# Attention with a bucketed bias and a snake feed-forward block: a new order of loads and units in the opening

## The chip, the cores and the metric

The kernel runs on one core of a Trainium2 chip. The metric is the device time of one execution in microseconds. A run of the kernel before took 372.21 us (median of three; 371.96 to 372.55).

## The reference

Eight batches, eight heads, 576 positions and a head size of 64: attention with a bias that depends on the distance of key and query alone, and then, over all 4608 rows of 512 numbers, a feed-forward block with the snake function.

```python
scores = q @ k.T / sqrt(64) + bias_table[bucket(|i - j|)]   # buckets: 32, one column a head
attn = softmax(scores)
x = (attn @ v) -> rows of all heads                          # 4608 x 512
h = x @ w_in                                                 # 512 -> 2048
g = h + sin(alpha * h) ** 2 / (alpha + 1e-9)
out = g @ w_out                                              # 2048 -> 512, float32
```

All distances from 128 on share the last bucket. So the exponential of a score is taken without bias, and only where a key lies within 128 positions of the query is it multiplied by the exponential of the bias (less that of the last bucket, which cancels in the softmax). These factors are the band rows.

## The kernel before, in words

**Names.** A batch is t (0 to 7); a pair p (0 to 3) is two heads. A pair's scores are transposed, keys on the partitions. The first 512 keys make four blocks c of 128, and such a unit is called A. The last 64 keys of both heads share one unit C. The last 64 queries have units of their own (B and X), which for the first batch are put off into the second batch. Every unit goes the same way: TensorE makes scores (L691, through the helper at L458), ScalarE takes the exponential into the tile `u` (L708), VectorE multiplies the part near the diagonal by the band rows `m2r` (L739), and for unit C VectorE or GpSimd does this with `mhr` (L725). Then TensorE multiplies with the values (`vs` for the first 512 keys, `vhs` for the last 64) and a column of ones, VectorE normalises (L953 and L954) into `xn`, TensorE transposes this for the first batch (L1025), and a copy puts it into `xT` (L538 on ScalarE, L540 on VectorE). The feed-forward block takes 512 rows of `xT` at a time: 16 groups of four matmuls with `w_in`, a sine on ScalarE (L1069), a square on ScalarE or VectorE (L1076, L1078), a sum on VectorE (L1083), and then four output tiles of 16 matmuls each with `w_out`, which may be put wherever TensorE would idle.

**The opening**, which is all the change touches directly. Batch 0's queries and keys come in pairs of heads. Pair 0 is loaded as float32 into `nat0` by SyncE (L433), cast into `natb` by `cast0` on VectorE (keys L468; queries half on VectorE, L516, half on GpSimd, L517), transposed by TensorE with an identity (L551) and copied to `kT` and `qT` by VectorE (L540). Pairs 1 to 3 come through GpSimd's queue, which casts on the way (`load_pair`, into `nat1`); pair 3 is issued later than the others. GpSimd copies the last 64 keys into `kts` (L582). The bias table goes through two small matmuls and an exponential (L596); the resulting 8 rows `e_sb` (L606) are written to DRAM (L607) and read back by SyncE with overlapping strides: `m2r` for heads 0-1, 2-3 and 4-7 (`load_m2r`, L474), and `mhr`, half-shifted rows for unit C, by two loads of their own (`load_mhr`, L481). The values of batch 0 come in three ways: heads 0 and 1 as float32 by SyncE at the very start into `vst` (L420), then cast by GpSimd (`cast_v`, L423); heads 2 and 3 through GpSimd's casting queue (L415); heads 4 to 7 as float32 by SyncE behind the band rows, and cast. `vst` lies in the memory of `w_out16`, so `w_out` can be loaded only after the casts. GpSimd then starts `w_in` (L439) once a one-element copy `tick` (L634) has seen the last band rows, clears the second set of tiles (`clear`), and loads batch 1's queries and keys into `nat2`, then `w_out` (L444), then batch 1's values.

**What sets the order.** A planner in the kernel's own Python code (`Plan`) holds tasks with the engines that may do them, a cost for each, dependences, a priority and a time before which a task isn't placed (`nb`; the constants `T_...`). It walks through its own estimate of time from `T_START`, gives each engine the ready task that can start first, and among those within 0.02 us the one with the lowest priority number. What comes out is a fixed order of instructions on each engine. At run time an engine waits at the head of its order for whatever its next instruction needs; nothing overtakes. In the first 22 us of the plan it also puts in products with a tile of zeros (`zz`, `warm1`), which only keep TensorE running.

## Time and profile before

| What | us |
|---|---|
| Median of three runs | 372.21 |
| The profiled execution | 372.11 |
| Span of its trace | 370.2 |
| TensorE busy | 362.5 |
| ScalarE busy | 316.8 |
| VectorE busy | 257.0 |
| GpSimd busy | 92.0 |

The trace starts with the first instruction of the program; the difference between span and time lies around it. PE is TensorE's matmul row, PEld its weight loads, DVE is VectorE, ACT ScalarE, POOL GpSimd, SP SyncE; a q behind a name is that engine's queue, issuing a DMA. A timeline row gives start and length in microseconds, engine, line of the kernel, operation, output and input by the program's names, shapes and a count, and in brackets how long the engine had been idle and what ended that. A window row gives a stretch and, for each engine, its busy time and number of instructions in it, then TensorE's granted clock, the share of the DMA engines and what they moved. A matmul's row is longer than the time it holds up the next one, as matmuls are pipelined. The granted clock is 1.00 all along.

### The profile page before, as it was taken

To read this page: it belongs to the slowest core of one execution; us is meant where nothing else is said; L and a number is where in the kernel's file an instruction comes from. 1 tells how busy PE (TensorE), PEld (TensorE's weight loads), DVE (VectorE), ACT (ScalarE), POOL (GpSimd) and SP (SyncE) were. 2 spreads that over 40 slices of the span, in tenths; PEclk is the share of its full clock that TensorE was granted. 3 is DMA by queue.
4 is the path that set the end of the run, shared out by engine and by line. 5 is a ranking of instruction groups with operands and counts; after the bars stand their busy time and mean duration, and the time that the engine had idled before them with its cause. 6 is when DMAs were issued, how large, how long until landed. Compare 5 with 4: busy or idle time off the path is not lost.

```text
span 370.2 us, 8922 instructions
## 1 busy us (share of the span) xinstructions
PE 362.5 (98%) x3576; PEld 195.7 (53%) x3576; DVE 257.0 (69%) x557; ACT 316.8 (86%) x433; POOL 92.0 (25%) x133
## 2 busy tenths in 40 slices
PE   7989999999999999999999999999999999999996
PEld 3564545644555446774554456445566455444443
DVE  4797957588677967696759776886769665979000
ACT  3998999899997999899979998999979997999111
POOL 7487450073000900073005600280005000000000
PEclk9999999999999999999999999999999999999999
DMA  9989999699525993399719991699259121000212
GB/s 169 199 160 205 201 163 147 132 90 141 99 58 109 122 161 71 86 134 143 119 48 146 141 145 53 135 115 171 68 105 104 61 69 37 7 28 4 84 60 86
DMA packets 149114, 40.49 MB, mean 109 GB/s; under 512 B 137080, under 2 KB 143568, under 8 KB 149072
## 3 DMA queue, kind: packets, MB, share of 16 engines
q0 software_dynamic: 96032, 17.67, 59.1%
q1 hardware_dynamic: 52864, 22.16, 25.4%
q8 instruction: 28, 0.46, 0.5%
q10 hardware_dynamic: 176, 0.09, 0.1%
q14 instruction: 14, 0.11, 0.1%
HBM read 37.73 MB, written 16.56 MB: 147 GB/s over the span
## 4 chain that ended last, share of the span: by engine, by line
PE 91%; ACT 5%; issue 1%; DVE 1%; ACTq 0%
PE pb L458 90%; ACT u L708 2%; ACT s L1069 1%; ACT sq L1076 1%; DVE u L739 1%; PE pb L1025 1%; PE pb L557 0%; ACT kT L538 0%; ACT qT L538 0%; DVE qT L540 0%; PE pb L551 0%; DVE xn L954 0%; DVE zz L509 0%; ACT outs L538 0%; DVE rd L953 0%
## 5 line engine op out<-in xcount | busy, mean ns | idle before, releaser
L708 ACT ACTIVATE u<-pb 128x1024 f16<-128x1024 f32 (+1 forms) x146 | 137.4, 1016 | 8.2 <-PE pb L458 6.7
L458 PE MATMUL pb<-w_out,g 128*128 128x512 f16 (+2 forms) x592 | 138.8, 374 | 0.0
L458 PE MATMUL pb<-xT,w_in 128*128 128x512 f16 (+4 forms) x704 | 127.6, 340 | 0.0
L1083 DVE SCALAR_TENSOR_TENSOR g<-sq,inv_a,pb 128x512 f16<-128x512 f16 x144 | 101.0, 743 | 7.1 <-ACT sq L1076 2.8
L1069 ACT ACTIVATE s<-pb,alphaT 128x512 f16<-128x512 f32 x144 | 93.0, 694 | 11.6 <-PE pb L458 10.8
L458 PEld LDWEIGHTS <-w_in 128*128 128x128 f16 x704 | 64.8, 98 | 57.4 <-issue 0.3
L739 DVE TENSOR_TENSOR u<-u,m2r 128x512 f16<-128x512 f16 (+1 forms) x128 | 62.2, 491 | 35.7 <-ACT u L708 32.5
L458 PEld LDWEIGHTS <-g 128*128 128x128 f16 x592 | 53.9, 98 | 59.9 <-issue 5.0
L458 PEld LDWEIGHTS <-u 128*128 128x128 f16 x1152 | 43.4, 97 | 10.4 <-issue 4.6
L403 POOL COPY kt<-kT 64x256 f16<-64x256 f16 x12 | 5.0, 421 | 171.2 <-DMA kT<-staged_k 86.3
L1076 ACT ACTIVATE sq<-s 128x512 f16<-128x512 f16 x71 | 44.4, 638 | 1.2 <-DVE g L1083 0.3
L458 PE MATMUL pb<-v,u 128*128 128x65 f16 x1024 | 44.1, 193 | 0.3 <-DVE u L739 0.3
L458 PE MATMUL pb<-qT,kT 64*128 64x64 f16 (+1 forms) x512 | 41.5, 285 | 1.5 <-ACT u L708 0.7
L1078 DVE TENSOR_TENSOR sq<-s 128x512 f16<-128x512 f16 x73 | 30.2, 423 | 12.4 <-ACT s L1069 11.5
L954 DVE TENSOR_TENSOR xn<-pb,rd 128x256 f16<-128x256 f32 (+2 forms) x59 | 28.5, 483 | 2.0
L458 PEld LDWEIGHTS <-kT 64*128 64x128 f16 x512 | 16.3, 94 | 22.9 <-issue 15.9
L458 PE MATMUL pb<-vh,u 128*128 128x130 f16 x128 | 28.2, 221 | 0.0
L408 POOL DMA_DIRECT2D v<-in_v_dram x28 | 24.8, 897 | 4.5 <-DMA nat<-in_k_dram 2.7
L538 ACT ACTIVATE outs<-pb 128x512 f32<-128x512 f32 (+2 forms) x12 | 6.8, 569 | 19.9 <-PE pb L458 19.9
L953 DVE RECIPROCAL rd<-pb 128x4 f32<-128x4 f32 (+2 forms) x59 | 10.9, 185 | 12.4 <-PE pb L458 12.3
L1148 ACT ACT_TABLE_LOAD x15 | 19.2, 1283 | 0.3
L540 DVE COPY outs<-pb 128x512 f32<-128x512 f32 x25 | 17.1, 685 | 3.2 <-PE pb L458 3.2
(75 smaller groups left out, 186.6 us busy)
## 6 DMA issues: line engine op xcount, KB each, us to landing
out_dram<-outs SPq DMA_DIRECT2D x35, 256.0 KB, 2.7
v<-in_v_dram POOLq DMA_DIRECT2D x28, 128.0 KB, 4.9
staged_k<-in_k_dram POOLq DMA_DIRECT2D x6, 576.0 KB, 9.1
staged_q<-in_q_dram POOLq DMA_DIRECT2D x6, 576.0 KB, 12.5
w_in<-in_moe_w_in_dram POOLq DMA_DIRECT2D x4, 512.0 KB, 8.7
w_out<-in_moe_w_out_dram POOLq DMA_DIRECT2D x4, 512.0 KB, 15.1
w_out<-in_v_dram SPq DMA_DIRECT2D x6, 128.0 KB, 6.2
xT<-xn SPq DMA_TRANSPOSE x47, 2.8
```

Source lines behind the costliest of these rows:

```text
L408: nc.gpsimd.dma_start(out=vs[t % 2][:, c, :, 0:D], in_=vp[128 * c : 128 * c + 128],)
L458: nc.tensor.matmul(out=out, lhsT=lhsT, rhs=rhs, start=start, stop=stop)
L540: k_of(e).tensor_copy(out=o, in_=i)
L708: nc.scalar.activation(out=o, in_=x, func=AF.Exp, scale=0.125)
L739: nc.vector.tensor_tensor(out=io, in0=io, in1=m2[:, 2 * p : 2 * p + 2, x0 : x0 + hi - lo], op=ALU.mult)
L953: nc.vector.reciprocal(out=r, in_=x[:, :, :, D])
L954: nc.vector.tensor_tensor(out=xn[:, 0:n].rearrange("p c (z d) -> p c z d", z=2), in0=x[:, :, :, 0:D], in1=r.unsqueeze(3).to_broadcast([128 ...
L1069: nc.scalar.activation(out=s16.v, in_=h.v, func=AF.Sin, scale=alphaT[:, f : f + 1])
L1076: nc.scalar.activation(out=sq.v, in_=s16.v, func=AF.Square)
L1078: k_of(e).tensor_tensor(out=sq.v, in0=s16.v, in1=s16.v, op=ALU.mult)
L1083: nc.vector.scalar_tensor_tensor(out=gcell[b].v[:, f, :], in0=sq.v, scalar=inv_a[:, f : f + 1], in1=h.v, op0=ALU.mult, op1=ALU.add,)
L1148: nc.scalar.preload_act_table_set(name)
```

## The change

All six loads of pairs 1 to 3 are issued by GpSimd at the start. The first queries are cast whole by VectorE. The copy of the first keys out of PSUM may be done by ScalarE alone. The two `mhr` loads are gone: GpSimd copies those rows out of `m2r`, in three pieces (pair 0, pair 1, pairs 2 and 3), each two instructions, and the multiplies of unit C wait for their piece. All eight heads' values of batch 0 come as float32 by SyncE, each pair of them behind the band rows of its heads, and GpSimd casts all eight; every product with values waits for its own heads' casts. `vhs` of batch 0 is loaded earlier on GpSimd's queue. `tick` waits for the middle band rows instead of the last; `w_in` is four tasks that other work may come between. The clears are split in three and due at 7.5 instead of 24.5. Batch 1's queries and keys wait for all casts, and `w_out` follows in a task of its own.

The planner gets a start for each engine, other due times and costs, and `HEAD_PRI`, priorities for single tasks of the opening. From the orders before and after: pair 1's keys are transposed ahead of the first scores. Pair 3's two copies on VectorE stand ahead of the first band multiply. The exponentials of unit C come one or two places sooner. Four feed-forward matmuls stand before the last pair's products instead of two. From there on the instructions are the same, apart from places of output matmuls, small copies that changed engine (batch 1's transposed keys and queries: six on ScalarE and two on VectorE, before five and three), and three output matmuls that stand before batch 1's first scores.

```diff
-        free = {e: t0 for e in ("PE", "ACT", "DVE", "POOL", "SP")}
+        free = dict(t0)
...
-T_START = 4.0
+T_START = {"PE": 4.7, "ACT": 3.6, "DVE": 6.05, "POOL": 5.6, "SP": 3.0}
-T_W0 = 24.5
+T_W0 = 22.6
-T_WI = 16.8
-T_CL = 24.5
+T_WI = 16.2
+T_CL = 7.5
-T_FIRST = (4.75, 5.95)
-T_PAIR = ((7.9, 8.5), (9.3, 10.2), (11.6, 12.3))
-T_M2 = (13.0, 14.8, 16.0, 16.0)
-T_MH = 14.2
-T_RST = 25.0
+T_FIRST = (4.97, 6.15)
+T_PAIR = ((6.6, 7.7), (8.7, 9.7), (10.7, 11.8))
+T_M2 = (13.1, 15.1, 18.0, 18.0)
+T_MH = (13.15, 15.15, 18.05)
+T_RST = 23.5
+T_V0 = (13.7, 14.3, 15.9, 16.5, 18.9, 19.5, 20.2, 20.8)
-T_TR1 = (36.0, 39.0)
-T_WO = (40.5, 43.0, 45.7, 48.3)
+T_TR1 = (33.2, 37.2)
+T_WO = (39.1, 41.7, 44.3, 47.4)
+HEAD_PRI = {0: 5618.9, 1: 5618.8, 3: 3520.2, ...}
...
-    def load_mhr(eng):
+    def copy_mhr(p0, p1):
         for z in range(2):
-            eng.dma_start(out=mhr[64 * z : 64 * z + 64], in_=bass.AP(tensor=e_dram, ...))
+            r, x = slice(64 * z, 64 * z + 64), 192 - 64 * z
+            P_.tensor_copy(out=mhr[r, p0:p1], in_=m2r[r, 2 * p0 + z : 2 * p1 : 2, x : x + 192])
...
-    load_v32(0)
-    load_v32(1)
...
-    load_pair(1)
-    load_pair(2)
+    for p in range(1, NP):
+        load_pair(p)
...
-    cast0(0, nc.vector)
-    x0 = nat0[:, 1].rearrange("s two (i d) -> s i two d", i=SI)
-    nc.vector.tensor_copy(out=natb[:, 1, :, 0], in_=x0[:, :, 0])
-    P_.tensor_copy(out=natb[:, 1, :, 1], in_=x0[:, :, 1])
+    for kq in range(2):
+        cast0(kq, nc.vector)
...
-            eng = {"ACT": 0.65} if p in T_ACT and kq else {"DVE": 0.75}
+            eng = {"ACT": 0.62} if p == 0 and not kq else {"DVE": 0.75}
...
-            load_m2r(nc.sync, 0, 2, 0)
-            load_mhr(nc.sync)
-            load_m2r(nc.sync, 2, 4, 3)
-            load_m2r(nc.sync, 4, H, 4)
-            for h in range(4, H):
-                load_v32(h)
+            for h0, h1, r in ((0, 2, 0), (2, 4, 3), (4, H, 4)):
+                load_m2r(nc.sync, h0, h1, r)
+                for h in range(h0, h1):
+                    load_v32(h)
...
+        for i, (p0, p1) in enumerate(((0, 1), (1, 2), (2, NP))):
+            x = plan.add({"POOL": ...}, lambda e, p0=p0, p1=p1: copy_mhr(p0, p1), [], 9000 + 3 * i, nb=T_MH[i])
+            mdone.extend([x] * (p1 - p0))
+        for h in range(H):
+            vdone.append(plan.add({"POOL": 0.45}, lambda e, h=h: cast_v(h), [], 9001 + 1.1 * h, nb=T_V0[h]))
+        for i in range(3):
+            plan.add({"POOL": 0.8}, lambda e, i=i: clear(P_, 1, i), [], 9900, nb=T_CL)
...
-            P_.tensor_copy(out=tick, in_=m2r[0:1, 4, 0:1])
+                if i == 0:
+                    P_.tensor_copy(out=tick, in_=m2r[0:1, 2, 0:1])
+                load_w_in16(i // 2, (2 * (i % 2),))
...
+        x = plan.add({"POOL": 1.7}, lambda e: load_nat2(), [], 9022, nb=T_RST, after=[x] + vdone)
+        x = plan.add({"POOL": 3.2}, lambda e: load_w_out16(), [], 9022, nb=T_RST, after=[x])
...
-                             ds + prev + (vdone[2 * y : 2 * y + 2] if t == 0 and p > 1 else []),
+                             ds + prev + (vdone[2 * p : 2 * p + 2] if t == 0 else []),
...
+    for i, x in HEAD_PRI.items():
+        plan.tasks[i].pri = x
     plan.run(T_START)
```

More of the change, by code (lines that the diff above doesn't have):

```diff
@@ L727, in bd @@
                 )
-            d = plan.add({"POOL": 0.45} if t == 0 and p else {"DVE": 0.25 if two else 0.15}, bd, [x],
-                         base + 10, nb=late, use=[ub])
+            d = plan.add({"POOL": 0.45} if t == 0 and p else {"DVE": 0.25 if two else 0.15}, bd,
+                         [x] + (mdone[p : p + 1] if t == 0 else []), base + 10, use=[ub])
             for pp in (p, p + 1) if two else (p,):
```

81 lines of the change are left out of this document (34 added, 47 removed), and 11 rows, old and new, of the table HEAD_PRI.

## Prediction

> **What bounds the kernel now.** I read the busy times of the page first, then windows, then single engines' timelines where the windows show a change of limit. TensorE has 98% of the span. The windows below cut it where the first feed-forward product is nearly complete (29.41) and where the second table load begins (46.30).
>
> ```profile
> PE 362.5 (98%) x3576; PEld 195.7 (53%) x3576; DVE 257.0 (69%) x557; ACT 316.8 (86%) x433; POOL 92.0 (25%) x133
> ```
>
> ```profile
> core 0: us, PE busy (x) PEld busy (x) DVE busy (x) ACT busy (x) POOL busy (x), PEclk, DMA share, GB/s
> 1.27:29.41 28.14, 25.70 (x327) 15.16 (x328) 20.70 (x57) 21.62 (x27) 19.88 (x45) 1.00 1.05 186
> 29.41:46.30 16.89, 16.36 (x191) 8.31 (x189) 14.78 (x27) 16.23 (x30) 8.70 (x14) 1.00 1.24 203
> 46.30:370.20 323.90, 320.48 (x3064) 172.24 (x3063) 221.18 (x473) 278.95 (x377) 62.87 (x71) 1.00 0.82 98
> ```
>
> After 46.30 TensorE is busy 320.48 of 323.90 us: that stretch is a fixed amount of work and moves only with its start. Before 29.41 TensorE's records hold warming products with the zero tile too, and run into each other, so they don't say what paces it. The change is worth what it moves the first sine (30.46) and everything behind it. Which engine paces the opening is seen in ScalarE's timeline and in the window from 15 to 20.
>
> ```profile
> 8.10 10.89 ACT L708 ACTIVATE u<-pb 128x1024 f16<-128x1024 f32 x12 [1.01 <-PE pb L458]
> 19.26 3.35 ACT L708 ACTIVATE u<-pb 128x1024 f16<-128x1024 f32 x4 [0.27 <-PE pb L458]
> 23.21 1.02 ACT L708 ACTIVATE u<-pb 128x1024 f16<-128x1024 f32 x1 [0.61 <-PE pb L458]
> ...
> 24.40 2.44 ACT L708 ACTIVATE u<-pb 128x512 f16<-128x512 f32 x3
> ...
> 30.46 0.69 ACT L1069 ACTIVATE s<-pb,alphaT 128x512 f16<-128x512 f32 x1 [0.47 <-PE pb L458]
> ```
>
> ```profile
> 15.00:20.00 5.00, 4.34 (x53) 2.37 (x51) 4.96 (x13) 4.74 (x6) 1.92 (x6) 1.00 0.84 199
> ```
>
> ScalarE works through twenty exponentials from 8.10 to 26.84 (24.40 + 2.44) with two stalls, 0.27 and 0.61, both for scores from TensorE. VectorE meanwhile is full, 4.96 of 5 us. TensorE takes its instructions in order: a product with the values that waits for VectorE's band multiply holds back the scores behind it, and so VectorE's backlog becomes ScalarE's stall. From the last exponential to the first sine are 30.46 − 26.84 = 3.62 us, a chain of multiply, product, normalisation, transpose and copy whose links the change leaves.
>
> **The change part by part.**
>
> *First exponential.* The first queries are now cast whole by VectorE, and the first of the copies out of PSUM goes to ScalarE.
>
> ```profile
> 4.30 0.56 DVE L468 CAST natx<-natx 96x768 f16<-96x768 f32 x1 [1.52 <-DMA natx<-in_k_dram]
> 5.47 0.36 DVE L516 CAST natx<-natx 96x384 f16<-96x384 f32 x1 [0.61 <-DMA natx<-in_q_dram]
> ```
>
> ```profile
> 5.50 0.69 POOL L517 CAST natx<-natx 96x384 f16<-96x384 f32 x1 [1.16 <-DMA natx<-in_q_dram]
> 6.50 0.59 ACT L606 ACTIVATE e_sb<-pb 8x512 f16<-8x512 f32 x1 [0.46 <-PE pb L458]
> L538 ACT ACTIVATE kT<-pb 128x576 f16<-128x576 f16 x3 | 2.1, 707 | 0.0
> 6.86 0.76 DVE L540 COPY qT<-pb 128x576 f16<-128x576 f16 x1 [0.37 <-PE pb L551]
> ```
>
> The queries were ready at 5.50 + 0.69 = 6.19 and will be at 5.47 + 0.56 = 6.03: −0.16. With the two value loads gone from beside them they may land a little sooner: I take −0.2, bounds 0 and −0.4. Pair 1's key transposes now stand before the first scores; what hides them is the copy of the first queries, which ended at 7.62 and will end near 7.4. If pair 1's keys land after that, every tenth counts. On ScalarE the key copy (0.71) stands ahead of e_sb, whose wait of 0.46 hides part of it: 0.71 − 0.46 = +0.25 for all band rows, bounds 0 and +0.4.
>
> *Band rows and VectorE.* This is the largest term: VectorE's timeline, then two landings from the list of DMA issues (its last number).
>
> ```profile
> 12.57 0.76 DVE L540 COPY qT<-pb 128x576 f16<-128x576 f16 x1 [0.16 <-PE pb L557]
> 14.72 0.43 DVE L739 TENSOR_TENSOR u<-u,m2r 128x512 f16<-128x512 f16 x1 [1.39 <-DMA m2r<-e_dram]
> 15.06 0.75 DVE L540 COPY kT<-pb 128x576 f16<-128x576 f16 x1
> 15.73 0.75 DVE L540 COPY qT<-pb 128x576 f16<-128x576 f16 x1
> 16.39 1.01 DVE L739 TENSOR_TENSOR u<-u,m2r 128x768 f16<-128x768 f16 x2
> ...
> 17.55 0.65 DVE L739 TENSOR_TENSOR u<-u,m2r 128x512 f16<-128x512 f16 x1
> ```
>
> ```profile
> 27.00 0.41 DVE L739 TENSOR_TENSOR u<-u,m2r 128x512 f16<-128x512 f16 x1
> ```
>
> ```profile
> 10.06 0.37 SPq L474 DMA_DIRECT2D m2r<-e_dram  x1
> m2r<-e_dram SPq DMA_DIRECT2D x1, 192.0 KB, 4.6
> nat<-in_k_dram POOLq DMA_DIRECT2D x1, 144.0 KB, 3.5
> ```
>
> VectorE idles 1.39 for the rows and only then, with multiplies due, does pair 3's two copies (1.5). With all keys and queries issued at once these copies can follow pair 2's, which ended at 12.57 + 0.76 = 13.33: by 14.1 to 14.8, so in the idle gap or nearly. The rows, issued at 10.06, landed 4.6 later; now issued near 10.3 with less beside them, they take between 3.5 (the quickest load of similar size, pair 3's keys) and 4.6: 13.8 to 14.9. I take 14.5 for the start of the multiplies, nearer the row of the same load. Pair 0's five took 0.43 for the first and 18.20 − 16.39 = 1.81 for the others, 2.24, so they end at 16.75 where they ended at 17.55 + 0.65 = 18.20: −1.45 before any cost.
>
> *What GpSimd now does there.* It gets six half-shift copies in place of two DMAs, casts eight value heads where it cast six, and does its clears early.
>
> ```profile
> 17.45 0.47 POOL L725 TENSOR_TENSOR u<-u,mhr 128x128 f16<-128x128 f16 x1 [1.08 <-DMA mhr<-e_dram]
> 18.96 0.18 POOL L634 COPY tick<-m2r 1x1 f16<-1x1 f16 x1 [1.04 <-DMA m2r<-e_dram]
> ...
> 22.08 0.44 POOL L423 CAST v<-w_out 128x256 f16<-128x256 f32 x1
> ```
>
> ```profile
> 23.50 0.76 POOL L423 CAST v<-w_out 128x256 f16<-128x256 f32 x1
> ```
>
> GpSimd's multiply at 17.45 lay under VectorE's at 17.55, which took 0.65 where the one at 27.00 took 0.41: 0.24 a meeting. Four casts and four copies now run from about 14 to 19, among the multiplies. A copy's length no row shows; the cast's 0.44 is the nearest. Three meetings make +0.7; the bounds are 0 and eight whole ones, 8 × 0.44 = +3.5. I stay low since the cast at 23.50, at 0.76, shows GpSimd waiting in its turn. VectorE's net is −0.75. The Trainium skill, SBUF — State Buffer, section "Who interferes with whom", says that a VectorE operation with two SBUF inputs and a GpSimd one that reads SBUF exclude each other for a whole instruction. Both long rows agree; by the rule alone the term lies nearer its upper bound, and that case is a rival below.
>
> *Values as float32 behind the rows.* Two casting loads on GpSimd's queue become SyncE loads, and the two that went out first now stand behind the first rows.
>
> ```profile
> w_out<-in_v_dram SPq DMA_DIRECT2D x1, 128.0 KB, 6.3
> w_out<-in_v_dram SPq DMA_DIRECT2D x1, 128.0 KB, 4.2
> 16.74 0.22 PE L458 MATMUL pb<-vh,u 128*128 128x130 f16 x1
> 18.83 0.39 PE L458 MATMUL pb<-qT,kT 64*128 64x512 f16 x2
> ```
>
> Issued at about 10.7 and 11.2 (0.37 an issue and its gap), they land 4.2 to 6.3 later, the second between 15.4 and 17.5; with its cast it is ready between 15.9 and 17.9. The middle, 16.9, lies beside multiplies that end at 16.75 + 0.7 = 17.45 with meetings: hidden unless near its upper end. The first product with values, at 16.74 before, starts no sooner, but meets no copies behind it. The last rows, for pairs 2 and 3, stand behind four value loads instead of two half-shift loads. GpSimd saw them land at 18.96; pair 2's multiplies need them soon after. I take +0.2, bounds 0 and +0.5.
>
> *Weights.* GpSimd started w_in after that wait at 18.96; it now waits for the middle rows, and has no clears between casts and the second batch. All these loads start 1 to 3 us earlier. No link of the chain to the first sine is a wait for w_in, so I count nil; it keeps them ahead of what moves earlier.
>
> *Sum.* ScalarE starts at −0.2. Of its 0.88 of stalls, VectorE's −0.75 takes as much, less part of the +0.2: −0.8 at most, together −1.0 for the last exponential and the first sine (29.5). Two more feed-forward matmuls run before the last transposes, in time TensorE idled, but from 29.41 to 46.30 ScalarE is busy 16.23 of 16.89 and gets one copy more (0.71), which earlier output matmuls cover. I count these two as nil, ±0.4. The profiled execution took 372.11 (span 370.2): 371.1. The median of the runs shown is 0.1 above it: **371.2**.
>
> **The rivals.**
>
> *A larger gain.* Rows and copies are there at 13.8 to 14.1, both stalls vanish, the extra matmuls and the earlier start count in full: −0.4 − 0.88 − 0.6 = −1.9, 370.3. For it: the idle 1.39 and the moved 1.5 are more than I credit. Against: ScalarE has 17.9 of work from first to last exponential without stalls, so no more than that can go.
>
> *A wash.* VectorE's gain comes, but the late e_sb (0.25), the last rows (0.3) and ScalarE's extra copy (0.3) eat all but 0.2: 372.0. For it: ScalarE is near full in both stretches.
>
> *Slower: the first values come late.* TensorE stands at the first product, in order, with the scores that ran at 18.83 behind it. The values decide from a landing of about 17.7 on: ready 18.1, product 18.1, scores near 18.8 as before. From there each us is a us for ScalarE. At 18.9, when the last rows landed on this queue, it costs 1.2: 373.4.
>
> *Slower: whole exclusion.* Eight GpSimd operations take 0.44 each from VectorE: +3.5 − 1.45 = +2.1 there, of which half reaches ScalarE past the time it has in hand: 373.2. Against: the long cast.
>
> **How the numbers follow.** Forecast 0.42, larger gain 0.18, wash 0.20, late values 0.10, whole exclusion 0.10. 0.2%, 0.74 us, is about what a measurement here can tell from no change. Faster: 0.39 of the forecast's 0.42 and the larger gain, 0.57. Same: the forecast's near edge, 0.03, the wash, and 0.02 of the two slower cases, 0.25. Slower: what is left of these two, 0.18. The range begins at the larger gain, 370.2, and reaches over the wash to the near side of the two slower cases, 372.9.
>
> **What would show it.** Right: the first band multiply near 14.5 with pair 3's copies before it, the last exponential ending near 25.8, the first sine near 29.5, and behind it the same distance to the end. Wrong: a first product with values that GpSimd's cast releases after 17.9; VectorE multiplies of 0.8 beside GpSimd copies; ScalarE stalls that add up to 0.9 again; or TensorE idle after 46 us that was not there.

## The result, and the profile after

The changed kernel takes 374.57 us (median of six runs, 373.43 to 375.19) beside 372.38 for the kernel before in the same runs: 1.0059 times as long, 95% interval 1.0039 to 1.0078. It is slower by 2.2 us; the forecast was 371.2, within 370.2 to 372.9. The profiled execution took 374.60 with a span of 372.9. Medians stand below because some executions, of the kernel before too (19 of its 122 beside the experiments), take 375 us or more; the last section shows one.

First the windows of the changed kernel, cut at the first sine, at the second table load and at the end, and then the window from 15 to 20 (columns as before).

```profile
core 0: us, PE busy (x) PEld busy (x) DVE busy (x) ACT busy (x) POOL busy (x), PEclk, DMA share, GB/s
1.27:31.32 30.05, 27.34 (x330) 15.78 (x331) 21.93 (x55) 22.78 (x30) 24.55 (x53) 1.00 0.95 176
31.32:47.94 16.62, 16.11 (x177) 7.60 (x177) 14.63 (x25) 16.51 (x29) 6.82 (x13) 1.00 1.24 201
47.94:372.88 324.94, 321.12 (x3082) 171.79 (x3073) 222.45 (x475) 277.64 (x375) 62.53 (x69) 1.00 0.81 98
15.00:20.00 5.00, 3.09 (x41) 1.82 (x40) 4.50 (x9) 3.98 (x5) 4.29 (x9) 1.00 1.10 257
```

The first sine is at 31.32 where it was at 30.46, and from the second table load to the end there are 324.94 us where there were 323.90. So 0.86 us were lost in the opening and 1.84 of the span behind the first sine (341.56 us to the end instead of 339.72): 1.04 in the stretch that the prediction held to be fixed, and the other 0.8 between the first sine and the second table load, called the sine stage below. It takes 16.62 us with 29 instructions on ScalarE. Here is its window in the kernel before, where there are 28:

```profile
30.46:46.31 15.85, 15.36 (x186) 7.93 (x185) 14.79 (x27) 15.80 (x28) 7.66 (x13) 1.00 1.25 202
```

ScalarE is busy for nearly all of both (16.51 and 15.80 us). ScalarE's timeline shows the opening.

```profile
8.48 9.76 ACT L711 ACTIVATE u<-pb 128x1024 f16<-128x1024 f32 x11 [1.02 <-PE pb L468]
19.26 1.02 ACT L711 ACTIVATE u<-pb 128x1024 f16<-128x1024 f32 x1 [1.01 <-PE pb L468]
20.71 3.35 ACT L711 ACTIVATE u<-pb 128x512 f16<-128x512 f32 x4 [0.43 <-PE pb L468]
24.24 2.43 ACT L711 ACTIVATE u<-pb 128x512 f16<-128x512 f32 x3 [0.18 <-PE pb L468]
...
26.90 1.02 ACT L711 ACTIVATE u<-pb 128x1024 f16<-128x1024 f32 x1
```

Three stalls add up to 1.62 us (1.01, 0.43, 0.18) where two made 0.88. Each is a wait for scores. TensorE's waits from 4 to 30 us have these longest rows (total, times, longest):

```profile
PE pb L468 <- DVE u L742: 1.0, 1, 1.0
PE pb L468 <- POOL v L430: 0.7, 1, 0.7
```

TensorE stood first for GpSimd's cast of the first values, then for a band multiply, with the scores behind. The band rows were read late: SyncE's row for the first read, its landing, and GpSimd up to the start of `w_in`.

```profile
11.65 0.40 SPq L484 DMA_DIRECT2D m2r<-e_dram  x1
m2r<-e_dram SPq DMA_DIRECT2D x1, 192.0 KB, 3.8
```

```profile
15.46 0.96 POOL L492 COPY mhr<-m2r 64x192 f16<-64x192 f16 x2 [1.28 <-DMA m2r<-e_dram]
16.48 0.82 POOL L430 CAST v<-w_out 128x256 f16<-128x256 f32 x2
17.25 1.15 POOL L492 COPY mhr<-m2r 64x192 f16<-64x192 f16 x2
18.48 0.47 POOL L728 TENSOR_TENSOR u<-u,mhr 128x128 f16<-128x128 f16 x1
18.91 1.39 POOL L430 CAST v<-w_out 128x256 f16<-128x256 f32 x2
20.24 0.18 POOL L637 COPY tick<-m2r 1x1 f16<-1x1 f16 x1
20.37 2.17 POOL L446 DMA_DIRECT2D w_in<-in_moe_w_in_dram  x3
```

The read was issued at 11.65, not near 10.3. GpSimd is then full from 15.46, and the weights, which were to start earlier, start at 20.37, 1.2 us later than before. Behind the first sine TensorE now has a wait on a load (from 30 to 60 us) that the kernel before does not have:

```profile
PE pb L559 <- DMA nat<-in_k_dram: 0.5, 1, 0.5
```

The chain that ended last changed as well. Its lines, of the kernel before and of the changed one:

```profile
PE 91%; ACT 5%; issue 1%; DVE 1%; ACTq 0%
```

```profile
PE 87%; DMA 7%; POOL 4%; ACT 0%; issue 0%; DVE 0%; ACTq 0%
PE pb L468 86%; DMA w_out<-in_moe_w_out_dram 5%; POOL v L430 1%; DMA e_dram<-e_sb 1%; DMA m2r<-e_dram 1%; POOL mhr L492 1%; POOL w_out L451 1%; POOL w_in L446 1%; PE pb L1028 0%; POOL nat L440 0%; POOL u L728 0%; ACT e_sb L608 0%; ACT kT L540 0%; PE pb L553 0%; DVE zz L514 0%
```

Before, the chain ran over ScalarE's work in the opening and the sine stage (ACT 5%). Now it runs over the write and read of the band rows, GpSimd's copies and casts, and then the loads of `w_in` and `w_out`: 5% of 372.9 is some 19 us behind a load of `w_out`.

### The profile page after: what moved, and what is told of

It reads as the page before. It is cut to its first block, busy times and chain, and to the rows that moved or that the text cites. A ratio compares the mean times of both kernels' runs of the same rounds, so it can differ in the third digit from the quotient of the medians.

```text
span 372.9 us, 8932 instructions
## 1 busy us (share of the span) xinstructions
PE 364.6 (98%) x3575; PEld 195.2 (52%) x3575; DVE 259.3 (70%) x556; ACT 316.9 (85%) x434; POOL 94.5 (25%) x138
## 3 DMA queue, kind: packets, MB, share of 16 engines
q1 hardware_dynamic: 53376, 22.23, 24.5%
## 4 chain that ended last, share of the span: by engine, by line
PE 87%; DMA 7%; POOL 4%; ACT 0%; issue 0%; DVE 0%; ACTq 0%
PE pb L468 86%; DMA w_out<-in_moe_w_out_dram 5%; POOL v L430 1%; DMA e_dram<-e_sb 1%; DMA m2r<-e_dram 1%; POOL mhr L492 1%; POOL w_out L451 1%; POOL w_in L446 1%; PE pb L1028 0%; POOL nat L440 0%; POOL u L728 0%; ACT e_sb L608 0%; ACT kT L540 0%; PE pb L553 0%; DVE zz L514 0%
## 5 line engine op out<-in xcount | busy, mean ns | idle before, releaser
L742 DVE TENSOR_TENSOR u<-u,m2r 128x768 f16<-128x768 f16 (+1 forms) x128 | 64.4, 507 | 37.8 <-ACT u L711 36.2
L468 PE MATMUL pb<-qT,kT 64*128 64x64 f16 (+1 forms) x512 | 42.6, 285 | 0.6 <-ACT u L711 0.5
L1081 DVE TENSOR_TENSOR sq<-s 128x512 f16<-128x512 f16 x72 | 29.9, 424 | 12.5 <-ACT s L1072 11.6
L540 ACT ACTIVATE outs<-pb 128x512 f32<-128x512 f32 (+2 forms) x10 | 5.5, 554 | 19.9 <-PE pb L468 19.9
L542 DVE COPY outs<-pb 128x512 f32<-128x512 f32 x27 | 18.5, 685 | 2.0 <-PE pb L468 2.0
L956 DVE RECIPROCAL rd<-pb 128x4 f32<-128x4 f32 (+2 forms) x59 | 11.0, 186 | 12.3 <-PE pb L468 10.8
```

Source lines behind the costliest of these rows:

```text
L468: nc.tensor.matmul(out=out, lhsT=lhsT, rhs=rhs, start=start, stop=stop)
L542: k_of(e).tensor_copy(out=o, in_=i)
L742: nc.vector.tensor_tensor(out=io, in0=io, in1=m2[:, 2 * p : 2 * p + 2, x0 : x0 + hi - lo], op=ALU.mult)
L956: nc.vector.reciprocal(out=r, in_=x[:, :, :, D])
L1081: k_of(e).tensor_tensor(out=sq.v, in0=s16.v, in1=s16.v, op=ALU.mult)
```

## The experiments

The theories, in the letters of the texts on record. **W**: the write of `e_sb` to DRAM is seen to land only when loads issued ahead of it have landed; six loads ahead of it instead of four make the band rows late. **G**: GpSimd's reads and VectorE's band multiplies exclude each other. **V**: the first values come late. **S**: TensorE's order behind the first sine is tied to the weights' stream (`w_in`, batch 1's rows, `w_out`), which starts later, while the due times put its users earlier. **C**: the exponential's cost in the plan, 0.055 instead of 0.065, worsens the order of the later batches. One text speaks of the late pair as a pair of values; it is pair 3's keys and queries.

### One suspect of the opening at a time

Late fourth pair (W), in the changed kernel:

```diff
-    for p in range(1, NP):
+    for p in range(1, NP - 1):
...
-            plan.add({"POOL": 0.8}, lambda e, i=i: clear(P_, 1, i), [], 9900, nb=T_CL)
+            plan.add({"POOL": 0.8}, lambda e, i=i: (load_pair(3) if i == 0 else None, clear(P_, 1, i)), [], 9900, nb=T_CL)
```

> The changed kernel, but pair 3's two loads are issued where GpSimd begins its early clears, just behind the write of the band rows to DRAM, as in the kernel before; all else in the same order. Theory W: that write is only seen to land when the loads issued ahead of it have landed (11.43 in the changed kernel, then the first read at 11.65; 9.91 and 10.06 before). Then the first read is issued near 10.2, 1.4 us sooner, the first band multiply starts near 14.1 to 14.5, and the time falls by 0.8 to 1.4 us, to 373.2 to 373.8. Theory G, GpSimd's copies slow VectorE and that is what costs: the read moves but the time falls by less than 0.5. If the write is late only because of its own later start (7.49 against 7.12), the first read stays near 11.6.

Half-shifted rows by two loads again, no GpSimd copies (G):

```diff
+                if h0 == 0:
+                    load_mhr(nc.sync)
...
-            x = plan.add({"POOL": ...}, lambda e, p0=p0, p1=p1: copy_mhr(p0, p1),
+            x = plan.add({"POOL": ...}, lambda e: None,
```

> The changed kernel with the half-shifted rows loaded by two DMAs behind the first band rows as before, and no GpSimd copies of them; all orders otherwise the same. Theory G, a GpSimd copy that reads the fast memory and a VectorE multiply exclude each other: the multiplies from 15.5 to 20 fall from 0.56 to 0.78 to about 0.45 to 0.6, the value casts end about 1 us sooner, and the time falls by 1 to 1.5 us. Theory W (the late write costs): the multiplies get shorter, but values and later rows now land 0.6 to 1 us later behind the two DMAs, and the time changes by less than 0.5.

First two value heads loaded at the very start again (V):

```diff
+    load_v32(0)
+    load_v32(1)
     nc.scalar.preload_act_table_set(EXP_SET)
...
-                for h in range(h0, h1):
+                for h in range(max(h0, 2), h1):
```

> The changed kernel with the value loads of heads 0 and 1 issued at the very start as before; the order of all engines the same. Theory V, the first product waits for late values: TensorE's wait of 0.71 for the cast goes and the time falls by about 0.7. Theories W and G: the product then waits for VectorE's multiply instead, which ended at 18.2 anyway, so the time stays within 0.3, or rises a little, as these loads land among the keys and queries (first queries 0 to 0.2 later).

The kernel before with all pairs issued at once (W from the other side):

```diff
     load_pair(2)
+    load_pair(3)
...
-        plan.add({"POOL": 1.4}, lambda e: load_pair(3), [], 9001, nb=T_P3)
+        plan.add({"POOL": 1.4}, lambda e: None, [], 9001, nb=T_P3)
```

> The kernel before with pair 3's two loads issued together with the others at the start, and nothing else: all orders stay. Theory W: the write of the band rows, issued at 7.1, is seen to land only behind them, near 11.2 to 11.5 instead of 10.06; band rows and first multiply come 1 to 1.4 us later, and the time rises by 0.7 to 1.4 us. Without W the transposes of pair 3 have their data sooner and the time stays or falls by up to 0.4.

Measured beside 372.42 (the ratios are estimated by themselves and are not quotients of the medians): 374.41 with the late pair (ratio 1.0045, 1.0010 to 1.0080), 374.79 with the loads (1.0045, 1.0014 to 1.0076), 375.27 with early values (1.0075, 1.0035 to 1.0115), and 373.97 for the kernel before with its pairs at once (1.0028, 1.0001 to 1.0055), 1.55 over it where 0.7 to 1.4 were expected. None of the three repairs brings the time back. What they did inside: the first row is the first read of band rows with the late pair, the second that of the kernel before with all pairs at once (10.06 without that edit).

```profile
9.54 0.41 SPq L484 DMA_DIRECT2D m2r<-e_dram  x1
```

```profile
12.30 0.37 SPq L474 DMA_DIRECT2D m2r<-e_dram  x1
```

W holds: the read moved by 2.1 us one way and 2.2 the other. With the late pair the first sine came at 30.32 instead of 31.32, and yet the time stayed: from first sine to end there were 342.29 us where the changed kernel has 341.56 and the kernel before 339.72. G's multiplies did shorten (the sixteen band multiplies sum to 8.85 us with the loads, 10.12 in the changed kernel, 8.15 before), and early values brought the wait for the cast from 0.7 to 0.4; neither moved the time down. So the opening's stalls are real, but taking them away one at a time does not bring the time back. TensorE's waits from 30 to 60 us with the late pair:

```profile
PE pb L559 <- DMA nat<-in_k_dram: 0.9, 1, 0.9
PE pb L468 <- DMA w_out<-in_moe_w_out_dram: 0.4, 1, 0.4
```

Most of the time won ahead of the first sine is spent waiting for batch 1's keys and for `w_out`. That led to S and C.

### The plan's constants and the stream

Planned cost put back from the second batch on (C):

```diff
-        x = plan.add({"ACT": n / 1200.0 + 0.055}, ex, ...)
+        x = plan.add({"ACT": n / 1200.0 + (0.065 if t else 0.055)}, ex, ...)
```

> The changed kernel with one constant of its planner put back for all batches but the first: the exponential's cost in the plan is 0.065 us again behind the opening (0.055 in the opening, as changed). No instruction is added or removed, only the order from the second batch on changes, back to that of the kernel before. Theory C (the cheaper exponential in the plan made every later attention stage order worse, 1.64 against 1.54 us of empty TensorE in each): the later stages come back to 1.54, the part from the second batch's first sine to the end is some 0.45 us shorter, and the time is 374.1 against the changed kernel's 374.5. Theory S (the weights come late for the plan, and TensorE stands in its order behind the opening) says nothing else changes: first sine at 31.3, last sine at 47.2, TensorE's stops for the first batch's weights as they were. Rival: the later stages are as full as they can be whatever the plan says, time unchanged within 0.2 us.

Late fourth pair, and due times put behind the landings (S):

```diff
-T_TR1 = (33.2, 37.2)
+T_TR1 = (36.3, 39.3)
-T_WO = (39.1, 41.7, 44.3, 47.4)
+T_WO = (41.4, 44.2, 46.8, 49.4)
```

> The changed kernel with the fourth values' pair loaded late (the version in which the first read of the band rows was issued at 9.54 and the first sine came at 30.3, but the time stayed at 374.4), and with the due times behind the first sine put back to when the weights land: second batch's transposes 36.3 and 39.3 instead of 33.2 and 37.2, output weights 41.4, 44.2, 46.8, 49.4 instead of 39.1, 41.7, 44.3, 47.4. Theory S (the opening's gain is given back because TensorE, which works in the written order, stands at products whose weights or rows have not landed): the stops of 0.95 us for the second batch's rows and of 0.4 us for the output weights go, TensorE's empty time between first sine and the second table load falls from 2.55 to some 1.7 us, and the time is 0.8 to 1.3 us shorter than with the late pair alone: 373.1 to 373.6. Rival: the stops are only moved, because nothing else is ready for TensorE there, then within 0.3 us of 374.4.

Both of these edits with the late pair:

> The version with the late pair and the due times put back, and with the exponential's planned cost at 0.065 again from the second batch on. Theories S and C add: 0.8 to 1.3 us from the first and 0.45 from the second, against 374.4: 372.6 to 373.2, about the kernel before. If both hold and the opening's 0.15 us at the first sine counts too, 372.3. If only C holds, 374.0; if only S, as the version without the cost put back, 373.1 to 373.6.

The kernel before with a later stream: two casts ahead of `w_in` on GpSimd.

```diff
             P_.tensor_copy(out=tick, in_=m2r[0:1, 4, 0:1])
+            for h in (4, 5):
+                cast_v(h)
```

> The kernel before with two of its casts of values on GpSimd moved ahead of the issue of the weights' stream, so that the stream starts some 1.1 us later, as it does in the changed kernel; nothing else is edited. Theory S (the stream takes some 30 us whenever it starts, and TensorE's order consumes its pieces as they land): first sine at 30.4 as before, the pieces of the output weights land 1.1 us later, TensorE stands for them, and the time is 0.7 to 1.1 us longer, 373.1 to 373.5. Rival: TensorE has other work in that stretch or the pieces are early anyway, under 0.3 us. If so, the changed kernel's later stream is no part of its loss, and only its earlier due times are.

Measured beside 372.09: cost alone 374.06 (1.0050, 1.0020 to 1.0079); due times 374.02 (1.0071, 1.0032 to 1.0110); both 373.02 (1.0029, 0.9989 to 1.0069); later stream 373.16, 1.07 over the median of before, though its ratio is open (1.0014, 0.9977 to 1.0050). Over the kernel before in the same runs, the late pair was at 1.99 us, with due times at 1.93, with both at 0.93. So the due times alone gave almost nothing there, against S's 0.8 to 1.3, the cost then 1.0, twice what C expected, and together they gave 1.06. The cost alone, with the changed opening, is at 1.97 where the changed kernel was at 2.19. A better order helps only where TensorE isn't standing for a load.

The traces price the planned cost by itself. From the third table load (the next one: 70.39 us before, 72.28 in the changed kernel) to the end of the trace there are 299.76 to 299.79 us in all eleven profiles of this document with the cost at 0.065, whatever came ahead, and 300.09 to 301.23 in the six with 0.055: 300.59 in the changed kernel, 299.78 with its cost put back. So the cost loses the changed kernel 0.8 us there, and the due times lose nothing there. In the run with the cost alone the gain does not show in the time, since 0.9 us went elsewhere, as follows.

The run with the cost alone has the changed kernel's orders on ScalarE, VectorE and GpSimd up to 68 us, and shows S by chance: its loads landed sooner, its first read came at 9.94 and its first sine at 30.40, 0.92 before the changed kernel's. Its waits from 28 to 62 us:

```profile
PE pb L468 <- DMA w_out<-in_moe_w_out_dram: 0.9, 1, 0.9
PE pb L559 <- DMA nat<-in_k_dram: 0.5, 1, 0.5
```

That is 1.4 us of waiting where the changed kernel has 0.5: the whole 0.9 is lost in front of the weights, and the third table load comes at 72.24, only 0.04 sooner. The kernel before with the later stream gets waits that it did not have:

```profile
PE pb L458 <- DMA w_out<-in_moe_w_out_dram: 0.5, 1, 0.5
PE pb L458 <- DMA w_in<-in_moe_w_in_dram: 0.3, 1, 0.3
```

The last piece of `w_out` is the place to look at: its issue and its landing time, of the kernel before and then of the changed kernel (the issues come in pairs in the timeline; the last starts at 31.35 and 31.17).

```profile
30.62 1.52 POOL L444 DMA_DIRECT2D w_out<-in_moe_w_out_dram  x2
w_out<-in_moe_w_out_dram POOLq DMA_DIRECT2D x1, 512.0 KB, 17.7
```

```profile
30.44 1.52 POOL L451 DMA_DIRECT2D w_out<-in_moe_w_out_dram  x2
w_out<-in_moe_w_out_dram POOLq DMA_DIRECT2D x1, 512.0 KB, 19.3
```

It lands at 49.08 before and at 50.44 after, though it was issued a little sooner after the change: from the start of `w_in` on the DMA engines are full (share 1.1 and above from 23 us on in both traces), and the stream takes 29.9 and 30.1 us from its first issue. Over the profiled executions, some of them of the runs in the next two parts (the sine stage with ScalarE's instructions in brackets; the product is the first one that waits for the last piece, counted from the landing; the difference is the time less the landing):

| kernel | first sine | sine stage | last `w_out` piece lands | its product | third table load | time | difference |
|---|---|---|---|---|---|---|---|
| before | 30.46 | 15.85 (28) | 49.08 | +0.04 | 70.39 | 372.11 | 323.03 |
| before, all pairs at once | 31.73 | 15.86 (28) | 51.03 | +0.04 | 72.34 | 374.05 | 323.02 |
| before, later stream | 30.95 | 15.83 (28) | 50.05 | +0.05 | 71.37 | 373.01 | 322.96 |
| late pair, both constants back | 30.19 | 16.73 (30) | 49.96 | +2.11 | 71.24 | 372.93 | 322.97 |
| changed | 31.32 | 16.62 (29) | 50.44 | +0.04 | 72.28 | 374.60 | 324.16 |
| changed, planned cost back | 30.40 | 16.57 (29) | 50.25 | +0.04 | 72.24 | 374.06 | 323.81 |
| late pair | 30.32 | 17.06 (29) | 50.17 | +0.04 | 72.02 | 374.46 | 324.29 |
| half-shifted rows by loads | 31.23 | 16.48 (29) | 50.63 | +0.04 | 72.48 | 374.28 | 323.65 |
| early values | 31.92 | 16.39 (29) | 49.87 | +0.74 | 72.42 | 375.21 | 325.34 |
| late pair, due times back | 30.02 | 16.73 (30) | 49.83 | +2.06 | 70.60 | 373.84 | 324.01 |
| before, changed due times | 30.60 | 15.91 (28) | 49.01 | +0.04 | 71.00 | 372.74 | 323.73 |
| before, changed planned cost | 34.22 | 15.86 (28) | 53.08 | +0.04 | 74.14 | 376.73 | 323.65 |
| changed, both constants back | 34.01 | 16.73 (30) | 53.83 | +2.05 | 75.05 | 376.82 | 322.99 |
| before, stream earlier | 30.27 | 15.84 (28) | 49.55 | +0.04 | 70.87 | 372.48 | 322.93 |

Two things can set the end, and the table tells them apart.

*The landing.* In the kernel before and its three variants with other loads (all pairs at once, later stream, stream earlier) the product starts as the piece lands; TensorE stood for it 0.02, 0.7, 0.5 and 0.7 us. The third table load follows the landing by 21.31 to 21.32 us, and the difference is 322.93 to 323.03, whatever the first sine was. So S is shown as a limit there.

*ScalarE's sine stage.* The two rows with both constants back have the same difference (322.97 and 322.99) but by coincidence: their product comes 2.1 us behind the landing, and no wait of TensorE is for it. What is longer there is the sine stage:

```profile
30.19:46.92 16.73, 16.02 (x185) 7.94 (x184) 14.77 (x25) 16.71 (x30) 6.72 (x13) 1.00 1.24 200
```

The planner has given ScalarE two squares more than in the kernel before (nine for seven), and VectorE two fewer. The stage goes by the number of ScalarE's instructions in every row: 28 take 15.83 to 15.91 us, 29 take 16.39 to 16.62 (17.06 with the late pair, where ScalarE idles 0.4), 30 take 16.73.

The changed kernel meets both limits at once. It has 29 instructions, the one copy more, and its landing is 1.36 us later; TensorE stood 0.08 us for the piece. So putting right one of the two alone gains next to nothing. With early values the product comes 0.74 behind the landing, so there it is not the landing that binds.

### How early can the stream come

> The kernel before with one index changed: the small copy that GpSimd makes from the band rows ahead of the weights' stream, to hold the stream back, reads a row of the middle load (landed 17.69) and not of the last (18.90). The order on every engine is the same. The stream starts some 1.0 us earlier (18.2 instead of 19.19) and by theory S its last output-weight piece lands 1.0 us earlier (48.1). Since in the kernel before TensorE's order already has its products behind the landings (no stop for a weight in the waits there), the time should fall by no more than the 0.27 us that its stage from the second table load to the next sine has over the later ones: 371.8 to 372.1. Rival A: profiled time less landing of the last piece was 323.0 in the four kernels with the same later order, so the time follows the landing all the way: 371.1. Rival B: the stream collides with the last band rows and the values (landing 18.9 to 20.7) and delays the opening: 372.3 to 373.

```diff
-            P_.tensor_copy(out=tick, in_=m2r[0:1, 4, 0:1])
+            P_.tensor_copy(out=tick, in_=m2r[0:1, 2, 0:1])
```

The same with the due times 1.0 us earlier (T_TR1, T_WO and batch 1's values):

> The same earlier stream in the kernel before, with the planner's due times for what the stream brings 1.0 us earlier each (second batch's transposes 35.0 and 38.0, output weights 39.5 to 47.3, next values 49.0), so that TensorE's order takes the weights earlier. Theory S: the time is 0.5 to 1.0 us under the kernel before, 371.1 to 371.6, since both the landing and the order move. Rival: the opening's exponentials and the first sine (30.46) set the stretch, not the stream; then within 0.2 us of the kernel before.

Late pair, cost back, the first piece of `w_in` ahead of the casts, due times in between:

```diff
-T_TR1 = (36.3, 39.3)
+T_TR1 = (34.8, 37.8)
-T_WO = (41.4, 44.2, 46.8, 49.4)
+T_WO = (39.9, 42.7, 45.3, 47.9)
...
-             lambda e, p0=p0, p1=p1: copy_mhr(p0, p1),
+             lambda e, p0=p0, p1=p1: (copy_mhr(p0, p1), None if p0 else load_w_in16(0, (0,))),
```

> The version with the late fourth pair, the planned cost put back and later due times (373.0), now with the first piece of the stream issued by GpSimd behind the first copies of half-shifted rows, near 15.1 us, and not behind the casts of four heads at 19.4; due times 1.5 us earlier (transposes 34.8 and 37.8, output weights 39.9 to 47.9). The other pieces stay where they were. Theory S: the last output-weight piece lands 1 to 2.5 us earlier (47.5 to 49.0 instead of 49.96), and the time falls by 0.8 to 1.2 us, to 371.8 to 372.2; the casts of the first two values come some 0.4 us later, which costs up to 0.4 of it. Rival: the piece takes the DMA engines from the last band rows and the values, the opening loses 0.5 to 1 us, and the time stays at 373.

The same with that piece behind the second cast:

> As the run with the first piece behind the first copies, but issued behind the first two casts of values (near 16.7 us), so that it holds up the second copies of half-shifted rows by 0.8 us and not the first values. Theory S: the last piece lands 1 to 2 us earlier than 49.96 and the time falls by up to 1.0 us, to 372.0; if the second pair's correction is on the path of the exponentials, 0.4 to 0.8 us of it are lost and the time is 372.4 to 372.8.

Measured beside 372.10: 372.40 (0.9993, 0.9964 to 1.0022), 373.92 (1.0017, 0.9982 to 1.0052), 372.69 (1.0009, 0.9971 to 1.0048) and 372.48 (0.9987, 0.9954 to 1.0021). The first three miss what was expected. The fourth lies in the range that its text gives should the second pair lose time; that it does is not shown. In the first, `w_in` was issued from 17.36 on, but the last piece landed at 49.55 and not at 48.1: batch 1's rows are issued behind casts and clears at 27.34, as before, and landed at 36.51. So the length of the stream is not a constant; its second half has an issue of its own. With due times set for an earlier landing that did not come (50.41), TensorE stood:

```profile
PE pb L458 <- DMA w_out<-in_moe_w_out_dram: 1.6, 1, 1.6
```

The two versions of the changed kernel with an early first piece do land sooner, at 48.55 and 48.02 instead of 49.96, and come down to where the measurement cannot tell them from the kernel before. The landing does not set the time there (the product comes 0.73 and 1.32 us behind it); TensorE's longest wait is another:

```profile
PE pb L468 <- DVE kT L542: 1.0, 1, 1.0
```

What they gained over the late pair with both constants back is not shown to come from the landing, which did not bind there either. Their sine stage has 29 instructions and takes 16.35 us instead of 16.73 with 30. In both, as in the two rows with both constants back, the third table load follows the second by 24.32 to 24.34 us, though the landing lies 21.22 to 22.81 ahead of it. Their first sines (30.08 and 30.14) are 0.3 to 0.4 us sooner than the kernel before's, and the longer stage takes 0.5 of it back. No version beats the kernel before beyond its interval.

### How much is opening, how much is plan

The changed kernel with its own opening and both constants back:

> The changed kernel with its own opening, all loads and copies as they are, and only planner constants changed back behind it: due times of the second batch's transposes 36.3 and 39.3 and of the output weights 41.4 to 49.4 (later, where they land), and the exponential's planned cost 0.065 from the second batch on. If the parts add (0.45 us for the cost, 0.4 to 0.7 for the due times, the rest for the opening's later landing of the last weight piece, some 1.1 to 1.4 us), the time is 373.3 to 373.6, with the last piece landing near 50.4 and the first sine near 31.2. If the opening is the whole loss: 374.2 or more. If the constants are the whole loss: 372.1 to 372.4.

The kernel before with the changed due times of batch 1's transposes and `w_out`:

> The kernel before with the changed kernel's due times for the second batch's transposes (33.2 and 37.2) and the output weights (39.1 to 47.4); opening and loads as before, last piece landing near 49.1. Theory S: TensorE's order now holds products ahead of their weights' landing by 0.5 to 2 us, it stands for them, and the time is 0.7 to 1.5 us over the kernel before: 372.8 to 373.6. Rival (the due times only shuffle work that is ready anyway): within 0.3 us of it.

The kernel before with the planned cost at 0.055 from the second batch on:

> The kernel before with the exponential's planned cost at 0.055 us from the second batch on, as the changed kernel has it; the opening and the first batch as before. Theory C: each later attention stage holds 1.64 us of empty TensorE instead of 1.54, and the time is 0.4 to 0.5 us over the kernel before: 372.5 to 372.6. Rival: no change within 0.2 us.

Measured beside 372.26: 373.32 (1.0036, 1.0008 to 1.0063), 373.56 (1.0038, 1.0023 to 1.0054) and 373.16 (1.0010, 0.9977 to 1.0044). With both constants back the changed kernel is 1.06 over the kernel before; of the 2.19 that it lost, 1.13 thus goes with the constants and 1.06 with the rest of the change. That rest is not the landing, as the table shows, and it lies behind the first sine: in this run's trace and in the late pair's with both constants back, the sine stage is 0.88 longer than before (16.73 for 15.85) and the way from the second to the third table load 0.24 longer (24.32 for 24.08, for which no run gives a reason); from there on they are equal to 0.02. The late pair's first sine is even 0.27 sooner than before; the usual first sine of this run is not on record, since its profile has the half-speed products of the last section. The late pair takes only 0.13 off the 1.06 (0.93), the earlier first piece of the stream another 0.3 to 0.6.

The due times alone cost the kernel before 1.30. This is within S's range, but the trace does not show S's mechanism: it is of the quickest of eight executions (372.74), and TensorE has no wait for a weight in it. The planned cost is not settled by the time (0.90 by the medians, but the interval holds 1); the trace has 300.74 us from the third table load on instead of 299.79, in C's direction and twice the 0.4 to 0.5 that was expected. Single prices do not add up: 1.30 and 0.90 exceed 1.13.

## Why the prediction was wrong

In the profiled executions the end came 3.5 us behind the forecast (374.60 for 371.1). Roughly, the first sine was 1.8 us late (31.32 for 29.5), the sine stage 0.8 longer and the stretch behind it 1.0 longer. The last two the prediction counted as nil.

**The sine stage: a step that failed.** ScalarE "gets one copy more (0.71), which earlier output matmuls cover. I count these two as nil, ±0.4." Output matmuls run on TensorE, and the prediction's own row had ScalarE busy 16.23 of 16.89 us there. Nothing covered the copy: from the start of a square or a copy to ScalarE's next instruction are some 0.53 us in this stage, and the stage grew by 0.77. (TensorE's wait of 0.5 us for batch 1's keys lies in this stage too, but ScalarE idled only 0.11 us in it.) No run takes that copy alone off the changed kernel; but in the kernel before with the stream earlier, the due times alone, set 1.0 us earlier, made it 29 instructions instead of 28 and 16.39 us instead of 15.84.

**Weights: a step that failed.** "All these loads start 1 to 3 us earlier. No link of the chain to the first sine is a wait for w_in, so I count nil." They start 1.2 us later (20.37 for 19.19), because the wait for the middle rows, gone at 17.17, was not what came last: the copies, a multiply and the casts on GpSimd's own queue were. And the argument looked for the load only ahead of the first sine. Behind it the last piece of `w_out` landed 1.36 us later, and TensorE came to it just then. By itself this cost 0.08 us of standing in the profiled execution; but whatever else had been put right would have been lost in front of it, as 0.9 us were in the run with the planned cost back.

**"A fixed amount of work" that "moves only with its start": a step that failed.** Its busy time says that TensorE is full, not that it starts when the sine does or that the order of its work stays as good. The stretch grew from 323.90 to 324.94; 0.8 of this is the planned cost, behind the third table load, and the prediction had no term for it. It took the other places of output matmuls and the earlier due times as nil; due times alone cost the kernel before 1.30 by the medians.

**First exponential.** Expected −0.2, profiled +0.38 (8.48 for 8.10). The same code gave 7.98 in the run with the planned cost back, so one profile cannot tell a term of 0.2 here. The queries were cast by 6.10 instead of 6.19, but their transposes went at 6.77 instead of 6.39, since the table's matmuls, which stand ahead of them in both kernels, ran later. What differs from execution to execution is when TensorE's products get fast. Those with 192 columns of zeros take 361 to 368 ns at first and 243 to 248 later; where no slow one of them was seen, the first exponential came at 7.84 to 8.16, and where the last slow one began at 5.46 to 6.12, at 8.34 to 8.48, in kernels of both kinds. The changed kernel's profile is of the second sort (6.12), the kernel before's lies between (4.82). So part of the late first sine belongs to the execution and not to the change.

**Band rows.** The length of the load was right (3.8 within 3.5 to 4.6), its issue not: "near 10.3" assumed that the issue hangs on `e_sb` alone. It goes with the loads issued ahead of the write: the last of them landed at 9.91 before and the read went out at 10.06; at 11.43 and 11.65 after; at 9.39 and 9.54 with the late pair (not counting a load issued 0.05 us ahead of the write, which landed at 10.91). It is not exact to the tenth: in the run with the cost back the read went out at 9.94, before a landing at 10.75. Pair 3's copies did move into the idle gap: they end at 14.31.

**GpSimd beside VectorE.** Three meetings for +0.7 were expected. VectorE's single multiplies from 15.5 to 20, the first and the last two:

```profile
15.50 0.71 DVE L742 TENSOR_TENSOR u<-u,m2r 128x768 f16<-128x768 f16 x1 [1.19 <-ACT u L711]
...
18.59 0.78 DVE L742 TENSOR_TENSOR u<-u,m2r 128x768 f16<-128x768 f16 x1
19.29 0.74 DVE L742 TENSOR_TENSOR u<-u,m2r 128x768 f16<-128x768 f16 x1
```

Against 0.55 for this form and 0.41 for the short one, the seven up to 20 us are longer by 1.2 in sum: the right mechanism, somewhat undersized, and far from the whole exclusion (+3.5). With the half-shifted rows loaded the multiplies were shorter and the time was not.

**Values.** Ready between 15.9 and 17.9 was right (second cast done at 17.30). "Hidden" was not: TensorE stood 0.7 for it. The rival of late values named this wait, but priced it by its delay of the first sine; loading them early did not help the time.

**Where the rivals stand.** The loss is of the size of the two slower ones, but for neither's reason: TensorE's wait for the values and the longer multiplies are in the trace, but shortening either did not help. The wash alone priced ScalarE's extra copy, at 0.3. Otherwise all rivals, like the forecast, were prices at the first sine, and this is the shared error: with the late pair the first sine moved by 1.0 us and the end by 0.14.

## What to carry to other kernels

A stage in which one engine is 98% busy is not by that a stage that starts when its input does: look for the loads that its written order depends on, and ask when their stream starts and ends under the change. A task on the queue that issues a long stream can delay the stream's end, even if it itself is hidden. Where a planner may move small operations between engines, count those of each engine stage by stage before and after: on an engine without idle time one more lengthens the stage. Two limits that are met at once hide each other, so a repair of one shows nothing. And a constant distance from a landing to the end is no proof that the end hangs on it: look whether the first user starts as it lands.

## What the runs showed of the hardware that was not expected

**A write waits for other queues' loads.** The small write of the band rows, issued by ScalarE between 6.8 and 7.7 us in the runs of this document, was seen complete (the first read went out) between 9.0 and 12.3 us, near the landing of loads that GpSimd had issued ahead of it, and followed them when one pair was moved. The Trainium skill, DMA: Bandwidth & Descriptors, section "Queues, rings and completion order" (HWDGE ordering), says that a completion increment is a strongly ordered write that lands only after every earlier write of that DMA engine, across its queues; the traces agree but for up to 0.8 us by which single reads went out before the last load had landed that was issued at least 0.2 us ahead of the write. The DMA engines were full at that time too (share 1.20 and above from 4 to 10 us in both kernels), and no run tells this ordering from the write waiting its turn.

**Half-speed products in some openings.** The run with both constants back was profiled in an execution of 376.82. The score products from 8 to 18 us (line, operation, shapes, count, busy us, mean ns), in the changed kernel and in that execution:

```profile
L468 PE MATMUL pb<-qT,kT 64*128 64x512 f16 x18 | 3.5, 384 | 0.5 <-ACT u L711 0.5
```

```profile
L468 PE MATMUL pb<-qT,kT 64*128 64x512 f16 x12 | 3.7, 605 | 0.0
```

A product took 605 ns instead of 384, up to about 20 us, with the granted clock at 1.00 in the profile's row all the time; the first sine came at 34.01. The planned-cost run of the kernel before was profiled in such an execution as well (376.73). The Trainium skill, TensorE: Matmul & The Clock Gate, Part 1, describes a gate that halves TensorE's clock until a window of activity of about 3.4 us has passed, at a phase that differs from run to run. Its figure for a single cold product of 512 columns (Part 2, Single matmul latency), (219 + 512) / 1.2 GHz = 609 ns, fits 605; a state that lasts to 20 us, with products of zeros from 1.3 us on, is far longer than that window. Why it strikes some executions stays open.
